# Decode attention, sixteen heads: V of the sixth pair loaded whole, a row selector built with one select, and the first load of K cut into 16 and 112 partitions

## The chip, the cores and the metric

The kernel runs on one core of one Trainium2 chip. The metric is device microseconds of one execution, as a median over runs. A profile of one execution is at hand too; its own time is given beside it below.

## The reference

One query row for each of 16 heads attends over 8192 keys; D is 256 and all data are bf16.

```python
B, H, Sq, Sk, D = 1, 16, 1, 8192, 256
scores = jnp.einsum("bhqd,bhkd->bhqk", q, k) * D ** -0.5
p = softmax(scores, axis=-1)
out = jnp.einsum("bhqk,bhkd->bhqd", p, v)
```

K and V are 64 MB each and each byte of them is used once.

## The kernel before, in words

The heads go in eight pairs, numbered 0 to 7. For one pair, head one lies on partitions 0 to 63 and head two on 64 to 127; each partition holds J = 128 consecutive keys of 256 elements, 64 KB. So the K of a pair is a transfer of 128 rows of 64 KB, 8 MB in all, and its V another. In the code `P` is 128, `HP` 64, `HJ` = J / 2 = 64, `NP` 8, `LAST` 7.

**The stream of loads.** All loads of K and V are issued by SP, one after the other, in the order that the string `ORDER` (line 17) gives: `k3` is K of pair 3, `v3` its V. A name in `parts` (line 100) is loaded in two halves of 32 KB a row, and the name with a plus is the second half. V of the last pair comes in five strips cut at `CUTS`. Line 136 issues each; lines 124 to 128 make SP wait first where the buffer is still in use. `kbuf` has room for two pairs, `vbuf` for one, so:

- a load of K of pair n waits until the K of pair n - 2 has been used by VectorE (semaphore `kd`) and GpSimd (`tp`);
- a load into the first half of `vbuf` waits until TensorE has used that half of the V before (semaphore `pa`);
- a load that reaches into the second half, a whole V among them, waits until TensorE has used all of the V before and made its total (semaphore `pr`). The test is `b <= HJ` in line 128.

SP runs its list in order, so a wait also holds up whatever comes later in `ORDER`. The semaphores `k0`, `k1`, `v` count the landing of whole transfers or of first halves (`k0` for even pairs, `k1` for odd), `kb`, `k7b`, `vb` that of second halves. Each transfer adds 16.

**The scores.** For each pair, GpSimd multiplies 24 keys of each half by q (line 215), ScalarE scales and sums these products (line 450), and VectorE does the other 40 keys of each half in one instruction per key (line 252). They start on a half of K when `k_waits` (line 149) and `side_wait` let them.

**The softmax and P times V.** When the scores of a pair are there, VectorE takes the maximum (`top`, line 234), TensorE turns it and spreads it (`turned`, line 292, `spread`, line 296), ScalarE makes the exponentials `E` (line 409). TensorE then multiplies `E` with the two halves of `vbuf`, 32 matmuls a half (`doubles`, line 319): it waits for semaphore `v`, does the first half, signals `pa`, waits for `vb`, does the second half, and `total` (line 307) signals `pr`. For the last pair only the first 92 keys go this way. TensorE then sums what it has so far over partitions (`gather`, line 341), adds the last 36 keys one by one (line 384), ScalarE and VectorE scale the row, and SP writes it out (lines 143 and 145).

**The small tables.** GpSimd builds `which` (2 x 128, in row r a one where the column belongs to head r) with a memset and two selects (lines 181 to 183), and then `ident` with a memset and one select. `which` is what TensorE needs, beside q, to spread the first q rows over the partitions (line 283).

Of the kernel before, what the change touches and what calls it, by code (L numbers as in the profile page):

```python
# [5 lines left out]
ALU = mybir.AluOpType  # L6
# [7 lines left out]
GRP = 3  # L14
CH = 8
SIDES = 2
ORDER = "k0 k0+ k1 v0 k2 v1 k3 v2 k4 v3 k5 v4 k6 k6+ k7 v5 v5+ k7+ v6 v6+ v7"
CUTS = (0, 64, 92, 112, 124)
LAST_PAIRED = 92
STRIP = 64  # L20
BLK = 32
ROWS = 98
AHEAD = {"sp": 2, "fin": 1, "rc": 2, "pr": 2, "pv": 2}
# [2 lines left out]
def bass_standalone__mha_softmax__decode_kernel(nc: bass.Bass, q: bass.AP, k: bass.AP, v: bass.AP, out: bass.AP):  # L26
    B, H, Sq, D = q.shape
    Sk = k.shape[2]
    P = 128
    NP = H // 2  # L30
    HP = P // 2
    J = Sk // HP
    HJ = J // SIDES
# [6 lines left out]
    HW = D // 2  # L40
    halves = ((0, 0), (BLK, HW))
    EW = 2 * J + BLK - 2
    LP = LAST_PAIRED
    LAST = NP - 1
    dt = k.dtype

    def pos(j):
        return j // BLK * (2 * BLK) + j % 2 * BLK + j % BLK // 2 * 2

    with contextlib.ExitStack() as ctx:  # L50

        def sb(name, shape, d):
            return ctx.enter_context(nc.sbuf_tensor(name, shape, d))
# [6 lines left out]
        def sem(name):  # L60
            if name not in sems:
                sems[name] = ctx.enter_context(nc.semaphore(name))
            return sems[name]
# [11 lines left out]
        which = sb("which", [2, P], dt)  # L75
# [9 lines left out]
        ones = small[:, 7:8]  # L85
        recip = small[0 : BLK + 2, 8 : 8 + NP]
        half = sb("half", [P, BLK + 2], FP32)
        negb = sb("negb", [P, 1], FP32)
        lsum = sb("lsum", [P, 1], FP32)
        ident = sb("ident", [P, P], FP32)  # L90
# [6 lines left out]
        spare = ps("spare", [P, 512])  # L97

        stream = []
        parts = {name: (0, HJ) for name in ("k0", "k6", "k7", "v5", "v6")}  # L100
        for name in ORDER.split():
            kind, n = name[0], int(name[1])
            if name == f"v{LAST}":
# [14 lines left out]
        def src(t, n):  # L118
            return t[0, 2 * n : 2 * n + 2].rearrange("h (p j) d -> (h p) (j d)", p=HP)

        @(lambda f: f(nc.sync))
        def _(sp):
            for kind, n, a, b, name in stream:
                if kind == "k" and n >= 2 and a == 0:
                    sp.wait_ge(sem("kd"), (n - 1) * NC)
                    sp.wait_ge(sem("tp"), (n - 1) * NG)
                elif kind == "v" and n >= 1 and a in (0, HJ):
                    sp.wait_ge(*((sem("pa"), n) if b <= HJ else (sem("pr"), n + 2)))
                if kind == "k" and n == 0 and a == HJ:
                    for late in ("k1", "kb", "k7b", "vb"):  # L130
                        sp.nop().then_inc(sem(late), 16)
                if kind == "k":
                    buf = kbuf[:, n % 2 * J * D :]
                else:
                    buf = vbuf
                sp.dma_start(buf[:, a * D : b * D], src(k if kind == "k" else v, n)[:, a * D : b * D]).then_inc(
                    sem(name), 16
                )
            sp.wait_ge(sem(stream[-1][-1]), 16)
            sp.wait_ge(sem("fin"), LAST + 1)  # L140
            flat = out.rearrange("b (n two) s d -> two (b n s) d", two=2)
            rows = qo[:, :].rearrange("t (n d) -> t n d", d=D)
            sp.dma_start(flat[:, 0:LAST, :], rows[:, 0:LAST, :]).then_inc(sem("o"), 16)
            sp.wait_ge(sem("fin"), LAST + 3)
            sp.dma_start(flat[:, LAST:NP, :], rows[:, LAST:NP, :]).then_inc(sem("o"), 16)
            sp.wait_ge(sem("o"), 32)
            sp.nop()

        def k_waits(e, h):
            e.wait_ge(sem("qb"), h + 1)  # L150
            e.wait_ge(sem("k0"), h // 2 * 16 + 16)
            e.wait_ge(sem("k1"), (h + 1) // 2 * 16 + 16)

        def side_wait(e, h, s):
# [4 lines left out]
        @(lambda f: f(nc.gpsimd))  # L159
        def _(pool):  # L160
            done = [0]

            def step(ins):
                done[0] += 1
                ins.then_inc(sem("pool"), 1)
                pool.wait_ge(sem("pool"), done[0])

            def keep(t, base, step_p, step_x, op, fill):
                step(
                    pool.affine_select(  # L170
                        out=t[:, :],
                        in_=t[:, :],
                        compare_op=op,
                        fill=fill,
                        base=base,
                        pattern=[[step_x, P]],
                        channel_multiplier=step_p,
                    )
                )

            step(pool.memset(which[:, :], 1.0))
            keep(which, 0, -HP, 1, ALU.is_ge, 0.0)
            keep(which, HP - 1, HP, -1, ALU.is_ge, 0.0)
            pool.nop().then_inc(sem("cb"), 1)
            for name, n in AHEAD.items():
                pool.nop().then_inc(sem(name), n)
            step(pool.memset(ident[:, :], 0.0))
            keep(ident, 0, 1, -1, ALU.not_equal, 1.0)
            step(pool.memset(ones, 1.0))
            step(pool.memset(half[:, :], 1.0))  # L190
            for c in (0, BLK):
                step(pool.memset(half[HP:P, c : c + 1], 0.0))
                step(pool.memset(half[0:HP, c + 1 : c + 2], 0.0))
            step(pool.memset(E[:, :], 0.0))
            for c in range(2):
                step(
                    pool.tensor_tensor(
                        out=sel[:, 2 * c : 2 * c + 2],
                        in0=ident[0:ROWS, c * BLK : c * BLK + 2],
                        in1=ident[0:ROWS, STRIP + c * BLK : STRIP + c * BLK + 2],  # L200
                        op=ALU.add,
                    )
                )
            pool.nop().then_inc(sem("cf"), 1)

            with pool.Fori(0, NP) as h:
                par = pool.snap(h % 2)
                with pool.Fori(0, SIDES) as s:
                    k_waits(pool, h)
                    side_wait(pool, h, s)  # L210
                    pool.nop().then_inc(sem("turn"), 1)
                    with pool.Fori(0, SG // 2) as i:  # L212
                        for b in range(2):
                            pool.wait_ge(sem("sp"), h * NG + s * SG + i * 2 + (b + 1))  # L214
                            pool.tensor_tensor(  # L215
                                out=prod[:, b * GRP * D : (b + 1) * GRP * D].rearrange("p (b d) -> p b d", b=GRP),
                                in0=kbuf[
                                    :, ds(par * (J * D) + s * (HJ * D) + i * (2 * GRP * D) + b * (GRP * D), GRP * D)
                                ].rearrange("p (b d) -> p b d", b=GRP),
                                in1=q_now[:, ds(par * D, D)].rearrange("p (b d) -> p b d", b=1).to_broadcast([P, GRP, D]),  # L220
                                op=ALU.mult,
                            ).then_inc(sem("tp"), 1)
# [58 lines left out]
        def _(pe):  # L281
# [33 lines left out]
            def doubles(a, b):  # L315
                for j in range(a, b, 2):
                    at = j // 2 % 2 * STRIP
                    x = pos(j)
                    ins = pe.matmul(  # L319
                        acc[at : at + STRIP, :],  # L320
                        lhsT=E[:, x : x + STRIP],
                        rhs=vbuf[:, j * D : (j + 2) * D],
# [33 lines left out]
            with pe.Fori(0, NP + 1) as h:  # L356
                par = pe.snap(h % 2)
                with pe.If(h > 0):
                    pe.wait_ge(sem("ex"), h)
                    pe.wait_ge(sem("v"), h * 16)  # L360
                    doubles(0, HJ).then_inc(sem("pa"), 1)
                    pe.wait_ge(sem("vb"), (h // (NP - 2) + h // LAST + h // NP) * 16 + 16)
                    doubles(HJ, LP)
                    with pe.If(h < NP):
                        doubles(LP, J)
                    total(h)
                with pe.If(h < NP):
                    pe.wait_ge(sem("m"), h + 1)
                    turned()
                    pe.wait_ge(sem("g"), h + 1)  # L370
                    spread()
                with pe.If(h < NP - 2):
                    qcast(back(h, -2), par)
                with pe.If(h > 0):
                    keep_running()
                    pe.wait_ge(sem("cm"), h)
                    pe.wait_ge(sem("fin"), h)
                    gather().then_inc(sem("pv"), 1)
# [124 lines left out]
```

## Time and profile before

| What | Value |
|---|---|
| Median of 3 runs | 316.98 us (316.96 to 317.62) |
| The profiled execution: its time | 317.37 us |
| Its span, from the first to the last instruction | 316.1 us |
| Bytes read from HBM | 134.23 MB |
| Busy: VectorE, GpSimd, ScalarE, TensorE | 225.6, 209.8, 194.6, 107.1 us |
| Share of the 16 DMA engines' span taken by SP's queue | 98.8% |

The span is 1.3 us shorter than the time of its own execution, and that execution took 0.39 us more than the median. In the page's second part each digit is a fortieth of the span, in tenths of busy time; the line for DMA is the mean over the 16 DMA engines. In the chain, each piece starts where the piece that released it ended; a DMA piece there runs from its issue to its landing, so it holds the time that the transfer stood in the queue behind others.

### The profile page before, as it was taken

The page shows a single profiled execution, that of the slowest core. Times are in us where ns is not written, and L with a number is a line of the kernel's source. Part 1 is how long each engine was busy: PE and PEld are TensorE (multiplying, and loading weights), DVE is VectorE, ACT ScalarE, POOL GpSimd, SP SyncE. Part 2 cuts the span into 40 slices and gives each one's busy share as a digit, 9 for nine tenths or more (in the row PEclk, how much of TensorE's full clock was granted, in tenths as well). Part 3 has the DMA queues.
Part 4 walks back from the last instruction along what each step waited for, and adds up shares of the span by engine and source line. Part 5 has one row for each costly group of instructions (what it writes and reads, how often), then busy time and mean ns, then how long its engine had stood idle before and what let it go on. Part 6 is the DMA issues. An engine that isn't in the chain of part 4 may idle for free.

```text
span 316.1 us, 7081 instructions
## 1 busy us (share of the span) xinstructions
PE 107.1 (34%) x718; PEld 46.8 (15%) x718; DVE 225.6 (71%) x1305; ACT 194.6 (62%) x840; POOL 209.8 (66%) x146
## 2 busy tenths in 40 slices
PE   0000000192005900069000790007700564258678
PEld 0000000041001400024000240002300122113335
DVE  0198989695596946969369692896989698969300
ACT  2066777766278653696537964468677967686541
POOL 3188888875486845858368582786888588868300
PEclk9999999997555785559755588555965558756779
DMA  8999999999999999999999999999999999999996
GB/s 333 402 460 456 473 398 398 489 440 398 398 398 531 398 398 398 531 398 398 489 440 398 398 531 398 398 398 464 398 464 398 464 398 464 398 464 406 456 400 267
DMA packets 3639, 134.25 MB, mean 425 GB/s; under 512 B 406, under 2 KB 438, under 8 KB 694
## 3 DMA queue, kind: packets, MB, share of 16 engines
q1 hardware_dynamic: 3620, 134.23, 98.8%
q8 instruction: 1, 0.02, 0.0%
q10 hardware_dynamic: 18, 0.01, 0.0%
HBM read 134.23 MB, written 0.01 MB: 425 GB/s over the span
## 4 chain that ended last, share of the span: by engine, by line
DMA 51%; POOL 16%; ACT 10%; PE 7%; issue 6%; ACTq 6%; POOLq 3%; SPq 0%
DMA kbuf<-in_k_dram 32%; DMA vbuf<-in_v_dram 19%; POOL prod L215 16%; ACT prod L450 8%; PE acc L319 6%; ACTq L450 4%; POOLq L215 2%; ACTq L446 2%; PE ob L384 1%; ACT E L409 0%; PE spare L330 0%; ACT comb L423 0%; POOLq L214 0%; POOLq L156 0%; POOLq L212 0%
## 5 line engine op out<-in xcount | busy, mean ns | idle before, releaser
L252 DVE SCALAR_TENSOR_TENSOR kbuf<-kbuf,qrow x640 | 219.9, 417 | 65.3 <-issue 65.3
L215 POOL TENSOR_TENSOR prod<-kbuf,q_now 128x768 f32 x128 | 207.0, 1639 | 83.5 <-ACT prod L450 46.3
L450 ACT ACTIVATE prod<-prod x384 | 155.3, 405 | 103.9 <-POOL prod L215 86.9
L319 PE MATMUL acc<-vbuf,E 128*64 128x512 bf16 x494 | 73.3, 468 | 15.7 <-DMA vbuf<-in_v_dram 12.7
L450 ACT ACTIVATION_READ_ACCUMULATOR prod<-prod x384 | 71.6, 186 | 0.0
L292 PE MATMUL mx<-ident,small 128*1 128x128 f32 x16 | 4.5, 380 | 176.2 <-DVE small L234 176.2
L252 DVE DVE_READ_ACCUMULATOR kbuf<-kbuf,qrow x640 | 52.8, 82 | 0.0
L319 PEld LDWEIGHTS acc<-vbuf,E 128*64 128x64 bf16 x494 | 33.0, 134 | 55.5 <-issue 25.8
L292 PEld LDWEIGHTS mx<-ident,small 128*1 128x1 f32 x16 | 0.7, 81 | 177.2 <-DVE small L234 177.2
L409 ACT ACTIVATE E<-S,negb 64x128 bf16 x16 | 13.9, 866 | 1.5 <-ACT negb L404 1.4
L330 PE MATMUL spare<-ident 128*128 128x512 f32 x16 | 14.7, 1016 | 0.1
L341 PE MATMUL ob<-comb,small 98*2 98x128 f32 x64 | 7.3, 373 | 9.9 <-ACT comb L423 9.9
L228 DVE RECIPROCAL small<-tot 34x1 f32 (+1 forms) x8 | 1.3, 159 | 10.8 <-PE tot L307 10.7
L423 ACT ACTIVATE comb<-acc 98x512 f32<-98x512 f32 x8 | 4.7, 593 | 6.2 <-PE tot L307 6.2
L409 ACT ACTIVATION_READ_ACCUMULATOR E<-S,negb 64x1 f32 x16 | 7.9, 494 | 0.0
L238 DVE TENSOR_REDUCE small<-mx 1x2 f32<-1x128 f32 x8 | 2.2, 279 | 7.0 <-PE mx L292 7.0
L341 PEld LDWEIGHTS ob<-comb,small 98*2 98x2 f32 x64 | 2.7, 99 | 22.0 <-ACT comb L423 21.0
L430 ACT ACTIVATE qo<-ob,small 2x128 f32 x14 | 4.9, 352 | 1.0 <-PE ob L341 0.9
L234 DVE TENSOR_REDUCE small<-S 128x1 f32 x8 | 2.3, 281 | 2.8 <-ACT prod L450 2.8
L296 PE MATMUL mx<-small 1*64 1x1 f32 x32 | 2.9, 244 | 3.0 <-DVE small L238 3.0
L330 PEld LDWEIGHTS spare<-ident 128*128 128x128 f32 x16 | 3.6, 279 | 1.4 <-issue 1.3
L283 PE MATMUL qrow<-qo,which 2*128 (+1 forms) x8 | 2.9, 391 | 2.6 <-DMA qo<-in_q_dram 2.4
(25 smaller groups left out, 19.9 us busy)
## 6 DMA issues: line engine op xcount, KB each, us to landing
kbuf<-in_k_dram SPq DMA_DIRECT2D x6, 4096.0 KB, 27.8
vbuf<-in_v_dram SPq DMA_DIRECT2D x5, 4096.0 KB, 23.7
vbuf<-in_v_dram SPq DMA_DIRECT2D x1, 1792.0 KB, 9.0
vbuf<-in_v_dram SPq DMA_DIRECT2D x1, 1280.0 KB, 11.7
vbuf<-in_v_dram SPq DMA_DIRECT2D x1, 768.0 KB, 13.1
vbuf<-in_v_dram SPq DMA_DIRECT2D x1, 256.0 KB, 13.3
kbuf<-in_k_dram SPq DMA_DIRECT2D x5, 44.1
vbuf<-in_v_dram SPq DMA_DIRECT2D x5, 27.9
```

What stands on the lines that cost most here:

```text
L215: pool.tensor_tensor(out=prod[:, b * GRP * D : (b + 1) * GRP * D].rearrange("p (b d) -> p b d", b=GRP), in0=kbuf[:, ds(par * (J * D) + s * ...
L252: ins = dve.scalar_tensor_tensor(out=col, in0=col, scalar=SCALE, in1=qrow[:, ds(par * 512, D)], op0=ALU.mult, op1=ALU.mult, accum_out=S[:, ...
L292: pe.matmul(mx[0:1, 0:P], lhsT=m[:, :], rhs=ident[:, :], start=True, stop=True).then_inc(sem("mT"), 1)
L319: ins = pe.matmul(acc[at : at + STRIP, :], lhsT=E[:, x : x + STRIP], rhs=vbuf[:, j * D : (j + 2) * D], start=(j < 4), stop=(j >= J - 4), s ...
L330: pe.matmul(spare[:, :].rearrange("p (b x) -> p b x", x=P), lhsT=ident[:, :], rhs=ident[:, :].rearrange("p (b x) -> p b x", b=1).to_broadc ...
L341: ins = pe.matmul(ob[row : row + 2, 0:HW], lhsT=sel[:, 2 * n : 2 * n + 2], rhs=comb[:, n * D + a : n * D + a + HW], start=(n == 0), stop=( ...
L384: ins = pe.matmul(ob[row : row + 2, 0:HW], lhsT=E[:, at : at + 2], rhs=vbuf[:, j * D + a : j * D + a + HW], start=False, stop=(j == J - 1) ...
L409: ins = act.activation(out=E[rows, 0 : 2 * J].rearrange("p (b two i t) -> p b i two t", b=J // BLK, two=2, t=2)[:, :, :, :, x], in_=S[rows ...
L423: act.activation(out=comb[:, :], in_=acc[0:ROWS, :], func=ACT.Copy).then_inc(sem("cm"), 1)
L430: ins = act.activation(out=qo[:, ds(i * D + a, HW)], in_=ob[row : row + 2, 0:HW], func=ACT.Copy, scale=recip[row : row + 2, ds(i, 1)],)
L446: with act.Fori(0, SG) as i:
L450: ins = act.activation(out=part, in_=part, func=ACT.Copy, scale=SCALE, accum_out=S[:, ds(par * J + s * HJ + i * GRP + b, 1)],)
```

## The change

Three things are done.

1. V of pair 5 (the sixth pair) is loaded in one transfer of 64 KB rows where it was two of 32 KB rows. Its one wait is that for a whole V, on `pr`. The threshold of TensorE's wait on `vb` loses the step that stood for this second half.
2. `which` is built with a memset of zeros and one select that puts a one where the row equals the head of the column. `ident` is built by the same helper, with the same operations as before.
3. The first half of K of pair 0, the first load of all, becomes two transfers on the same semaphore: partitions 0 to 15, and then partitions 16 to 127. The threshold of the wait on `k0` rises by 16.

```diff
-ORDER = "k0 k0+ k1 v0 k2 v1 k3 v2 k4 v3 k5 v4 k6 k6+ k7 v5 v5+ k7+ v6 v6+ v7"
+ORDER = "k0 k0+ k1 v0 k2 v1 k3 v2 k4 v3 k5 v4 k6 k6+ k7 v5 k7+ v6 v6+ v7"
...
+FIRST = 16
...
-        parts = {name: (0, HJ) for name in ("k0", "k6", "k7", "v5", "v6")}
+        parts = {name: (0, HJ) for name in ("k0", "k6", "k7", "v6")}
...
-                sp.dma_start(buf[:, a * D : b * D], src(k if kind == "k" else v, n)[:, a * D : b * D]).then_inc(
-                    sem(name), 16
-                )
+                rows = ((0, FIRST), (FIRST, P)) if (kind, n, a) == ("k", 0, 0) else ((0, P),)
+                for lo, hi in rows:
+                    sp.dma_start(
+                        buf[lo:hi, a * D : b * D], src(k if kind == "k" else v, n)[lo:hi, a * D : b * D]
+                    ).then_inc(sem(name), 16)
...
-            e.wait_ge(sem("k0"), h // 2 * 16 + 16)
+            e.wait_ge(sem("k0"), h // 2 * 16 + 32)
...
-            step(pool.memset(which[:, :], 1.0))
-            keep(which, 0, -HP, 1, ALU.is_ge, 0.0)
-            keep(which, HP - 1, HP, -1, ALU.is_ge, 0.0)
+            ones_where_zero(which, [[-1, 2], [0, HP]])
...
-            step(pool.memset(ident[:, :], 0.0))
-            keep(ident, 0, 1, -1, ALU.not_equal, 1.0)
+            ones_where_zero(ident, [[-1, P]])
...
-                    pe.wait_ge(sem("vb"), (h // (NP - 2) + h // LAST + h // NP) * 16 + 16)
+                    pe.wait_ge(sem("vb"), (h // LAST + h // NP) * 16 + 16)
```

The new helper:

```python
def ones_where_zero(t, pattern):
    step(pool.memset(t[:, :], 0.0))
    step(
        pool.affine_select(
            out=t[:, :], in_=t[:, :], compare_op=ALU.not_equal, fill=1.0,
            base=0, pattern=pattern, channel_multiplier=1,
        )
    )
```

More of the change, by code (lines that the diff above doesn't have):

```diff
@@ L166, in step @@
                 pool.wait_ge(sem("pool"), done[0])
-            def keep(t, base, step_p, step_x, op, fill):
+            def ones_where_zero(t, pattern):
+                step(pool.memset(t[:, :], 0.0))
                 step(
@@ L172, in keep @@
                         in_=t[:, :],
[L173 to L177, printed above, removed]
-                    )
-                )
-            step(pool.memset(which[:, :], 1.0))
-            keep(which, 0, -HP, 1, ALU.is_ge, 0.0)
-            keep(which, HP - 1, HP, -1, ALU.is_ge, 0.0)
+                        compare_op=ALU.not_equal,
+                        fill=1.0,
+                        base=0,
+                        pattern=pattern,
+                        channel_multiplier=1,
+                    )
+                )
+            ones_where_zero(which, [[-1, 2], [0, HP]])
             pool.nop().then_inc(sem("cb"), 1)
```

## The prediction

> **What bounds the kernel now.** I read the page first: the busy lines, the line of DMA slices, and the table of DMA queues.
>
> ```profile
> span 316.1 us, 7081 instructions
> ...
> DMA  8999999999999999999999999999999999999996
> ...
> q1 hardware_dynamic: 3620, 134.23, 98.8%
> ```
>
> No engine of the core is busy for more than 71% of the span, but the sixteen DMA engines are full in every slice except the first and the last. Then I asked for windows: the start in small pieces, and one long stretch of the middle (the last two columns are the share of the DMA engines and GB/s; a packet is counted whole where it starts, so a short window can show more than 1).
>
> ```profile
> core 0: us, PE busy (x) PEld busy (x) DVE busy (x) ACT busy (x) POOL busy (x), PEclk, DMA share, GB/s
> 0.00:1.72 1.72, 0.00 (x0) 0.00 (x0) 0.00 (x0) 0.34 (x1) 0.97 (x7) 1.00 0.00 0
> 1.72:1.82 0.10, 0.00 (x0) 0.00 (x0) 0.00 (x0) 0.10 (x1) 0.00 (x0) 1.00 0.15 46
> 1.82:2.02 0.20, 0.00 (x0) 0.00 (x0) 0.00 (x0) 0.20 (x1) 0.00 (x0) 1.00 6.59 1820
> 2.02:12.90 10.88, 0.60 (x2) 0.12 (x2) 0.00 (x0) 1.03 (x2) 1.82 (x11) 1.00 0.94 401
> 20.00:300.00 280.00, 94.13 (x572) 40.01 (x572) 219.52 (x1272) 186.19 (x816) 201.90 (x125) 0.70 1.00 432
> ```
>
> From 20 to 300 us the share is 1.00 at 432 GB/s: nothing in the core ever lets the queue run dry. The stream starts at 1.82. The chain of waits shows how it hangs together at both ends (start, length, what):
>
> ```profile
> 0.81 12.09 DMA kbuf<-in_k_dram
> ...
> 75.90 44.08 DMA kbuf<-in_k_dram
> ...
> 153.08 44.30 DMA kbuf<-in_k_dram
> ...
> 230.87 24.72 DMA vbuf<-in_v_dram
> 255.63 5.61 PE acc L319 x32
> 261.26 23.48 DMA vbuf<-in_v_dram
> 284.78 6.39 PE acc L319 x32
> 291.18 12.97 DMA vbuf<-in_v_dram
> 304.20 6.71 PE acc L319 x46
> 310.95 1.05 PE spare L330 x2
> 312.00 0.54 PE ob L341 x8
> 312.54 2.03 PE ob L384 x72
> 314.59 0.36 ACT qo L471
> ```
>
> Here the reader is to see two things. The end is set by the landing of the first half of the last V, 291.18 + 12.97 = 304.15, and 10.8 us of TensorE, ScalarE and output behind it. And every landing is set by the queue: a transfer lands when those ahead of it are through, however early it was issued. So the whole kernel is a pipe of fixed length. An edit pays, one for one, only if it starts the pipe sooner, shortens the sum of its transfers, or opens a gap in it.
>
> **The unit of the sum.** Halves first: from the landing of the first half of V5 (230.87 + 24.72 = 255.59) to that of V6 (261.26 + 23.48 = 284.74) three halves pass: 29.15 / 3 = 9.717 us each. Wholes: from K3 (75.90 + 44.08 = 119.98) to K5 (153.08 + 44.30 = 197.38) four pass, V2, K4, V3, K5: 77.40 / 4 = 19.35 us each. A half has 128 rows on 16 engines, eight rows an engine, so a 32 KB row takes 9.72 / 8 = 1.21 us of its engine, which moves 432 / 16 = 27 GB/s.
>
> **Part 1, V5 whole.** Two halves cost 2 x 9.717 = 19.43 us, a whole 19.35: the gain is 0.08 us of pipe. The bounds are 0 and 0.1, for both landings are read to hundredths. What it costs lies in waits, so these rows come next: SP's issues, and TensorE around V5.
>
> ```profile
> 227.38 0.20 PE L307 MATMUL tot<-lsum,half 128*34 128x1 f32 x2
> ...
> 230.50 0.33 SPq L136 DMA_DIRECT2D kbuf<-in_k_dram  x1
> 230.87 0.43 SPq L136 DMA_DIRECT2D vbuf<-in_v_dram  x1
> ...
> 265.34 5.33 PE L319 MATMUL acc<-vbuf,E 128*64 128x512 bf16 x32 [4.12 <-DMA vbuf<-in_v_dram]
> 270.51 0.20 PE L307 MATMUL tot<-lsum,half 128*34 128x1 f32 x2
> 277.37 0.59 PE L292 MATMUL mx<-ident,small 128*1 128x128 f32 x2 [6.66 <-DVE small L234]
> ...
> 284.78 0.64 PE L319 MATMUL acc<-vbuf,E 128*64 128x512 bf16 x2 [0.86 <-DMA vbuf<-in_v_dram]
> ```
>
> - SP's wait: the whole V5 waits for `pr`, given at 227.58 by the total of V4. SP only reaches V5 at 230.87, after waiting for K5 to be used up. The new wait is over 3.3 us before it is asked, and behind it in SP's list stands only the second half of K7, which now goes out one issue sooner.
> - TensorE: it can no longer start V5 at 255.63 with the first half; it waits for the whole, about 255.59 + 19.35 - 9.72 = 265.2. The first 32 matmuls then take what such a batch took, 5.33 to 6.39 us, so `pa` comes at 270.6 to 271.6 instead of 261.24, and SP issues the first half of V6 that late. The second half of K7 keeps the engines at work until 265.2 + 9.7 = 274.9, and an issue needs 1.82 - 0.81 = 1.01 us to its first data. So V6 must be issued by 273.9: a cover of 2.3 us at the worst batch.
> - TensorE's second batch ends at 275.9 to 278.0. The next thing it has to do is the turn at 277.37, so that is at most 0.7 late; TensorE idles 0.86 us before V6, which swallows it. The second half of V6, issued on `pr` by 278.3, is needed at about 283.6.
>
> So the whole of part 1 is -0.08 us.
>
> **Part 2, one select less.** GpSimd, and who waits for it:
>
> ```profile
> 1.07 0.63 POOL L170 TENSOR_SCALAR_AFFINE_SELECT which<-which 2x128 bf16<-2x128 bf16 x2
> 2.43 0.60 PE L283 MATMUL qrow<-qo,which 2*128 2x256 bf16 x2 [2.43 <-DMA qo<-in_q_dram]
> 14.33 3.23 POOL L215 TENSOR_TENSOR prod<-kbuf,q_now 128x768 f32 x2 [9.54 <-issue]
> ```
>
> Two selects took 0.63, so about 0.3 us go. But TensorE's first matmuls waited for q, not for `which` (done at 1.70), and GpSimd itself idles 9.54 us before its first product. Worth 0; without that cover it would be a gain of 0.3. A select over two dimensions could be slower than the plain one; the cover takes that in too.
>
> **Part 3, 16 rows ahead of 112.** This part has the only large unknowns. The first issue, the shortest one of the run, and one that directly follows another:
>
> ```profile
> L136 SPq DMA_DIRECT2D kbuf<-in_k_dram x1: 405/405/405, 0.8 to 0.8; - x1
> ...
> 314.97 0.28 SPq L145 DMA_DIRECT2D out_dram<-qo  x1
> ...
> 231.82 0.43 SPq L136 DMA_DIRECT2D kbuf<-in_k_dram  x1
> ```
>
> The first issue runs from 0.81 to 1.22 and the data start at 1.82, 0.60 later. A transfer with 2 rows was issued in 0.28, so with 16 rows at best 0.41 - 0.28 = 0.13 us go. If the 0.60 us of hand-over too shrank with the rows, to 16 / 128 of it, 0.53 us more would go: the far end of the gain is 0.66. The near end is 0: the trace has no 16-row load and an issue of 0.43 for 128 rows, so the count of rows may not matter. I take 0.13, since the two-row issue is the only row that is close in size.
>
> On the cost side, the second transfer is issued behind the first, by 1.22 + 0.05 + 0.43 = 1.70 at the latest, and has data 0.60 later, at 2.30. An engine has its first row of 1.21 us until 1.69 + 1.21 = 2.90 at the earliest, so there is no hole; without that cover it would cost the second issue, 0.48. The extra completion costs nothing that I can see: the halves against wholes above, with eight more rows an engine and a completion more, differ by 0.08 in all, so I take +0.01. All loads behind are issued 0.5 later, with 10 us of queue ahead.
>
> What the trace does not bear out is that sixteen neighbouring rows can be written at the full 432 GB/s. At full rate, one row an engine, they take 1.21 us and the pipe stays as long. The nearest rows: a 128-row load writes eight rows per engine's share of 27 GB/s. If a row group keeps just that share, sixteen rows have two shares and take 8 x 1.21 = 9.7, a loss of 8.5 us. Against that, the q load in the window 1.72 to 1.82 put 46 GB/s into two neighbouring rows, more than the one share of 27. It is a tenth of a microsecond and a few KB, which a buffer may have taken, but it is the only narrow write here, and I take it: no loss.
>
> [...]
>
> **The sum.** On the profiled execution: 317.37 - 0.08 - 0.13 + 0.01 = 317.17. That execution was 0.39 above the median of the runs, so against the median 316.98 - 0.20 = 316.78, say 316.8 us. A change of less than 0.2%, 0.63 us, is about what a measurement of this kernel cannot tell from none.
>
> **The rivals.**
>
> - *Narrow writes, slower.* Sixteen neighbouring rows share a part of the write side, and the first rows hold all sixteen engines, whose queues are in order. [...] If the 112 rows, seven to an engine, also fall unevenly, the loss grows towards the 8.5 of two shares: up to 325.3. It decides as soon as the first rows take more than 0.8 us longer than 1.21. For it: the eight rows per share above, and a pipe with no slack to hide it. Against it: the q load.
> - *The split does nothing.* The data start at 1.82 as before, and only 0.08 is left: 316.9.
> - *The hand-over shrinks too.* -0.66 - 0.08: 316.2, faster. Against it: 0.60 us after an issue is also what a mere latency would look like.
> - *V6 comes late.* If TensorE's first batch on V5 took over 8.7 us, the queue would dry up after K7, one for one. The rows say 5.3 to 6.4, so even 10 us would cost just 1.3: 318.1.
>
> **How the numbers follow.** The forecast has 0.47, the split that does nothing 0.10, the narrow writes 0.33 (0.20 near 320.4, 0.13 towards 325), the hand-over 0.07, a late V6 0.03. Within 0.2%: 0.47 + 0.10 = 0.57. Slower: 0.33 + 0.03 = 0.36. Faster: 0.07. The range runs from 316.2, the full hand-over, to 321.0, which takes in the loss of 3.6 and a little more; what lies beyond, 0.13 and some at the edges, is under 0.2. The forecast's own range is 316.3 to 317.4.
>
> **What would show it.** In the profile after, the first half of K0 should land at about 12.8 (12.90 before), the stream should show 432 GB/s from then on, and the first half of the last V should land near 303.9. [...] V5's matmuls should come as one batch of 64 from about 265, `which` with one select of some 0.3 us. A DMA share under 1.00 between 273 and 277 would show a late V6. The prediction is wrong if the first rows are slow, or if the start moves by more than 0.6 us.

## The result, and the profile after

| | Before | After |
|---|---|---|
| Median | 316.98 us (5 runs, 316.93 to 317.62) | 327.42 us (5 runs, 326.7 to 327.82) |
| The profiled execution: its time, its span | 317.37, 316.1 us | 326.7, 324.8 us |

The ratio is 1.0311, with a 95% interval of 1.0294 to 1.0327: the change costs 10.4 us by the medians. The profiled execution after is the fastest of its five, so the two profiled executions lie 9.3 us apart, and what makes up the other 1.1 no profile shows. The forecast was 316.8 us, no difference that can be measured, with a range from 316.2 to 321.0. It was wrong.

The page of the kernel after, its first line, the DMA slices and the rate in each slice, and then the rate in the kernel before:

```profile
span 324.8 us, 7080 instructions
...
DMA  8999998999999989989989999999999998999996
GB/s 134 291 291 448 500 404 387 500 404 396 500 396 412 492 387 460 444 387 500 404 387 500 404 396 500 396 412 428 444 420 428 452 460 383 444 444 404 444 401 253
```

```profile
GB/s 333 402 460 456 473 398 398 489 440 398 398 398 531 398 398 398 531 398 398 489 440 398 398 531 398 398 398 464 398 464 398 464 398 464 398 464 406 456 400 267
```

The line of DMA slices looks nearly the same as before. The rate does not: for the first three slices, 24 us, the engines are about as busy as before and move 134 to 291 GB/s, where they moved 333 to 460. Section 6 of the page has the landing of the 16 rows, 7.1 us after their issue at 0.74, so at 7.84:

```profile
kbuf<-in_k_dram SPq DMA_DIRECT2D x1, 512.0 KB, 7.1
```

Windows cut at the landings show the same (last two columns: share of the DMA engines, GB/s):

```profile
core 0: us, PE busy (x) PEld busy (x) DVE busy (x) ACT busy (x) POOL busy (x), PEclk, DMA share, GB/s
1.72:7.84 6.12, 0.60 (x2) 0.13 (x2) 0.00 (x0) 1.26 (x2) 1.84 (x11) 1.00 1.07 173
7.84:22.24 14.40, 0.00 (x0) 0.00 (x0) 0.00 (x0) 0.00 (x0) 0.00 (x0) 1.00 1.00 275
22.24:31.96 9.72, 0.00 (x0) 0.00 (x0) 7.94 (x47) 4.79 (x23) 7.20 (x5) 1.00 1.06 455
40.00:300.00 260.00, 86.52 (x536) 36.71 (x536) 206.45 (x1197) 173.60 (x758) 189.31 (x118) 0.68 1.00 433
```

Between 7.84 and 22.24 the share is 1.00 at 275 GB/s: each engine has a packet under way, but the packets get on slowly (1.5 to 3.2 us for a row of the 112, where a row takes 1.21 at 432 GB/s). From 22 us on, the rate is what it was. The chain of waits of the kernel after (start, length, what):

```profile
1.18 21.06 DMA kbuf<-in_k_dram
...
161.89 44.22 DMA kbuf<-in_k_dram
...
239.67 34.28 DMA vbuf<-in_v_dram
273.95 0.04 issue
273.99 8.63 PE acc L320 x64
...
282.68 20.41 DMA vbuf<-in_v_dram
...
309.38 12.72 DMA vbuf<-in_v_dram
...
322.14 1.08 PE ob L385 x32
...
323.24 0.36 ACT qo L472
```

The first half of the first K lands at 1.18 + 21.06 = 22.24 in place of 12.90: 9.34 us late. K of pair 5 lands at 206.11 in place of 197.38: 8.7 late. The span is 8.7 us longer too. So the whole loss in the trace is made before 22 us, and the pipe hands it on to the end. The 0.6 us between 9.34 and 8.7 lie between the landings of the first half of K and of K3, 107.08 us before (12.90 to 119.98) and 106.47 after (22.24 to 128.71). The loads between are the same, and two profiles of one kernel below differ there by more, 106.46 and 107.45, so this is a difference between executions.

The two small parts came out as worked out. V of the sixth pair runs as one batch of 64 matmuls, after its landing at 273.95. From the landing of K5 at 206.11 to there pass V4 (19.35), three halves of K (29.15) and V5, which leaves 19.34 us for it: 0.09 less than two halves. The first half of V6 is asked for at 279.20, 4.5 us before the second half of K7 is in (273.95 + 9.72 = 283.67):

```profile
279.20 31.09 SPq L139 DMA_DIRECT2D vbuf<-in_v_dram  x7
```

The select, and the matmuls that wait for q, in the timeline after:

```profile
1.17 0.28 POOL L174 TENSOR_SCALAR_AFFINE_SELECT which<-which 2x128 bf16<-2x128 bf16 x1 [0.24 <-POOL which L172]
...
3.98 0.60 PE L284 MATMUL qrow<-qo,which 2*128 2x256 bf16 x2 [3.98 <-DMA qo<-in_q_dram]
```

One select takes 0.28 us. The q rows are there 1.55 us later than before (2.43); nothing needs them before 22 us.

### The profile page after: what moved, and what is told of

It reads as the page before. It is cut to its first block, busy times and chain, and to the rows that moved or that the text cites. A ratio compares the mean times of both kernels' runs of the same rounds, so it can differ in the third digit from the quotient of the medians.

```text
span 324.8 us, 7080 instructions
## 1 busy us (share of the span) xinstructions
PE 103.9 (32%) x718; PEld 45.5 (14%) x718; DVE 225.6 (69%) x1305; ACT 195.1 (60%) x840; POOL 209.7 (65%) x145
## 4 chain that ended last, share of the span: by engine, by line
DMA 54%; POOL 15%; ACT 9%; issue 6%; ACTq 6%; PE 5%; POOLq 3%; SPq 0%
DMA kbuf<-in_k_dram 33%; DMA vbuf<-in_v_dram 21%; POOL prod L216 15%; ACT prod L451 8%; PE acc L320 4%; ACTq L451 4%; POOLq L216 2%; ACTq L447 1%; SPq L139 0%; ACT E L410 0%; PE ob L385 0%; ACT comb L424 0%; POOLq L215 0%; POOLq L159 0%; POOLq L213 0%
## 5 line engine op out<-in xcount | busy, mean ns | idle before, releaser
L320 PE MATMUL acc<-vbuf,E 128*64 128x512 bf16 x494 | 70.4, 454 | 21.9 <-DMA vbuf<-in_v_dram 18.8
L320 PEld LDWEIGHTS acc<-vbuf,E 128*64 128x64 bf16 x494 | 32.0, 130 | 59.8 <-issue 22.6
L399 ACT ACTIVATE q_now<-qrow (+1 forms) x8 | 3.1, 382 | 2.0 <-PE qrow L284 1.8
```

The costliest lines, as they stand in the source:

```text
L320: ins = pe.matmul(acc[at : at + STRIP, :], lhsT=E[:, x : x + STRIP], rhs=vbuf[:, j * D : (j + 2) * D], start=(j < 4), stop=(j >= J - 4), s ...
L399: act.activation(out=q_now[:, ds(at * D, D)], in_=qrow[:, ds(at * 512, D)], func=ACT.Copy).then_inc(sem("qb"), 1)
```

## The experiments

The theories, as they stood before the runs. *Shared write paths*, an assumption that no trace had shown: neighbouring partitions share a way into the memory, so rows that go to few of these ways are slow, and they hold up all engines, whose queues are in order. Against it: the loss belongs to the *start of the stream*, or to *one transfer more*, or to a transfer with *few rows*, or to the *read* of neighbouring rows in HBM, or in part to *V in one transfer*.

**The first K whole again.**

```diff
-rows = ((0, FIRST), (FIRST, P)) if (kind, n, a) == ("k", 0, 0) else ((0, P),)
+rows = ((0, P),)
...
-e.wait_ge(sem("k0"), h // 2 * 16 + 32)
+e.wait_ge(sem("k0"), h // 2 * 16 + 16)
```

> Only the split of the first load is undone; V of the sixth pair stays in one transfer and the row selection keeps its one select. If the split carries the whole loss, the time is that of the kernel before less the 0.08 us that the prediction gave to V in one transfer: 316.9 us. If V in one transfer, or the select, has a part in the 10.4 us, what is left of the loss shows here: any time over 317.6, the slowest run of before.

Measured: 317.29 us beside 317.52 of the kernel before, ratio 0.9998 (0.9977 to 1.0019). The loss is gone. The runs spread further, though: seven lie at 316.7 to 317.4 and five at 317.9 to 320.0. In the kernel that cuts along the keys, below, on the same chip, four of ten lie at 319.4 to 320.5; the kernel before has one of 23 above 319 there. That is taken up below. In its chain the first half of K lands at 0.74 + 12.12 = 12.86:

```profile
0.74 12.12 DMA kbuf<-in_k_dram
...
152.46 44.26 DMA kbuf<-in_k_dram
230.22 34.34 DMA vbuf<-in_v_dram
```

**The split alone**, in the kernel before, with V in two halves and two selects.

> The kernel before with the split of the first load alone; V of the sixth pair stays in two halves and the selector in two selects. The extra loads by themselves cost 3.1 us over full rate for the 16 rows and 6.2 us for the 112. If the split is the whole loss, 9.3 us more than before and little spread, about 326.7. If V in one transfer has a share of its own in the 10.4 us, this kernel is faster than the changed one by that share, about 1 us.

Measured: 327.32 us beside 317.36, ratio 1.032 (1.03 to 1.0339). The changed kernel had 1.0311. So the split carries all of the loss, and the other two parts have none of it, within 0.2%. In its chain the first half of K lands at 1.25 + 21.59 = 22.84, 9.9 us late:

```profile
1.25 21.59 DMA kbuf<-in_k_dram
```

**Two transfers, cut along the keys.**

```diff
-rows = ((0, FIRST), (FIRST, P)) if (kind, n, a) == ("k", 0, 0) else ((0, P),)
+cols = ((0, 8), (8, HJ)) if (kind, n, a) == ("k", 0, 0) else ((a, b),)
...
-buf[lo:hi, a * D : b * D], src(k if kind == "k" else v, n)[lo:hi, a * D : b * D]
+buf[:, lo * D : hi * D], src(k if kind == "k" else v, n)[:, lo * D : hi * D]
```

> The first half of the first K still comes in two transfers, but cut along the keys: 8 keys and then 56 keys, each over all 128 rows. Shared write paths (neighbouring rows share a way into the memory, and the engines' queues are in order): all rows are written side by side again, so no loss, about 317 us and the half landed at about 12.9 us. A cost of starting the stream with two transfers: the loss stays, 8 to 10 us, so 325 to 327.

Measured: 317.37 us beside 317.52, ratio 1.0015 (0.9989 to 1.004). The half is there at 1.20 + 12.40 = 13.60, 0.7 us later than in one transfer, so it gains nothing, but the 9 us are not there. Two transfers at the start of the stream are not the cause.

```profile
1.20 12.40 DMA kbuf<-in_k_dram
```

**The same cut, in the middle of the stream.**

```diff
-rows = ((0, FIRST), (FIRST, P)) if (kind, n, a) == ("k", 0, 0) else ((0, P),)
+rows = ((0, FIRST), (FIRST, P)) if (kind, n, a) == ("k", 6, 0) else ((0, P),)
...
-e.wait_ge(sem("k0"), h // 2 * 16 + 32)
+e.wait_ge(sem("k0"), h // 2 * 16 + 16 + h // 6 * 16)
```

> The cut into 16 and 112 rows is made at the first half of the seventh K, some 225 us into a running stream; the first K is whole. Shared write paths: the same rows meet the same paths, so 8 to 10 us more again, 325 to 327. If the loss belongs to the start of the stream, 316.9. If it is a fixed cost of one transfer more, it must already be hidden by a full queue: under 317.5.

Measured: 328.38 us beside 317.52, ratio 1.0325 (1.0288 to 1.0362). In its chain K5 still lands at 197.12 (196.72 with the first K whole), and V5 at 275.65 in place of 264.56:

```profile
152.56 44.56 DMA kbuf<-in_k_dram
230.61 45.04 DMA vbuf<-in_v_dram
```

A window of the same kernel over the stretch between the two:

```profile
core 0: us, PE busy (x) PEld busy (x) DVE busy (x) ACT busy (x) POOL busy (x), PEclk, DMA share, GB/s
223.00:237.00 14.00, 4.61 (x46) 2.35 (x40) 7.04 (x42) 7.14 (x32) 6.49 (x4) 0.84 0.94 267
```

The same picture as at the start: the engines nearly full, at 267 GB/s. The loss goes with the rows, not with the start. From K5 to V5 it is 78.53 us in place of 67.84, so 10.7 more; why that is 1.4 above the loss at the start, no run here tells.

**64 and 64 rows.**

```diff
-FIRST = 16
+FIRST = 64
```

> The first half of the first K is cut into rows 0 to 63 and 64 to 127. If the loss comes from a transfer of very few rows, it should nearly go, since each has half of all rows: under 318. Shared write paths: 64 neighbouring rows reach only a part of them, and at half of the paths each transfer takes as long as the whole one, 9.72 us twice in place of once: +9.7, 326.6 us. [...]

Measured: 328.08 us beside 317.52, ratio 1.0327 (1.0299 to 1.0355); the half lands at 1.35 + 22.41 = 23.76, 10.9 us late. Two transfers of half the rows take some 10 us each, as long as one with all rows. So it is not the small number of rows in the first transfer that costs the time.

```profile
1.35 22.41 DMA kbuf<-in_k_dram
```

**Sixteen rows by themselves**, in three ways. The first K is whole; ahead of it go 16 extra rows into the buffer of V, and V's first load waits for them.

```diff
+sp.dma_start(vbuf[0:16, 0 : HJ * D], src(k, 0)[0:16, 0 : HJ * D]).then_inc(sem("x"), 16)
 for kind, n, a, b, name in stream:
+    if kind == "v" and n == 0:
+        sp.wait_ge(sem("x"), 16)
```

> The first K is whole again; ahead of everything SP loads 16 rows of the first K once more, into partitions 0 to 15 of the buffer of V, which is loaded over them later. So the cost of a 16-row transfer stands by itself. Full rate, one 32 KB row an engine: 1.21 us, the first half of K lands at 12.9 + 1.2 = 14.1 us. [...]

Every eighth partition: `vbuf[0:121:8, ...]`.

> The same 16 rows of K, but written to every eighth partition (0, 8, 16 to 120) in place of 0 to 15. [...]

Every eighth row of HBM: `src(k, 0)[0:121:8, ...]`.

> Partitions 0 to 15 are written as in the first of these four, but with every eighth row of K from HBM in place of 16 neighbouring ones. [...]

Measured, in this order, beside 317.41 us: 321.11, ratio 1.0118 (1.0097 to 1.0139); 319.36, 1.0063 (1.0042 to 1.0084); 321.38, 1.0124 (1.0103 to 1.0145). The chains, one fence each, give the landing of the first half of K: 17.15, 15.48 and 17.43, where 12.86 is the value without extra rows.

```profile
1.18 15.97 DMA kbuf<-in_k_dram
```

```profile
1.39 14.09 DMA kbuf<-in_k_dram
```

```profile
1.18 16.25 DMA kbuf<-in_k_dram
```

So, by the landings, 16 rows cost 4.3 us in neighbouring partitions and 2.6 us in partitions that lie eight apart, from the same rows of HBM; other rows of HBM into the same partitions, 4.6. At full rate it would be 1.21. By the medians the three cost 3.7, 2.0 and 4.0 us, in the same order. So what decides here is which partitions are written: 4.3 and 4.6 us for 0 to 15, 2.6 for every eighth.

The traces also have the time of each packet, and each row of 32 KB is one packet (128 packets for each of the eleven loads of 32 KB rows in the kernel before). In the first half of K of the kernel before, a row takes 1.21 to 1.3 us from the second row of each engine on, and 1.3 to 2.2 for each engine's first. The 16 neighbouring rows take 3.2 to 4.5 us each (3.0 to 4.4 in the changed kernel), the 16 rows eight apart 1.8 to 2.5, and the rows of the two transfers of 64, after the first, 2.4 to 2.6.

**The 112 rows by themselves**, in the same way.

> The same with rows 16 to 127, 112 of them, seven an engine, ahead of the whole first half. Even use of the paths: 7 x 1.21 = 8.49 us, the half of K lands at 21.4. [...]

Measured: 331.62 us beside 317.41, ratio 1.0446 (1.0424 to 1.0467). The half lands at 27.55, so 112 rows took 14.7 us: 6.2 more than 8.49. Its packets are slow throughout: each of the seven rows of an engine takes 1.6 to 2.8 us.

```profile
1.18 26.37 DMA kbuf<-in_k_dram
```

The books close by the landings: 4.3 - 1.2 = 3.1 for the 16 rows and 6.2 for the 112 make 9.3; the changed kernel's first half landed 9.34 late, that of the split alone 9.9. By the medians the same sum is 2.5 + 5.7 = 8.2, less than the 10.0 to 10.4 of the two kernels with the split, so the close fit holds for these profiles and not for every run. Either way some two thirds of the loss lies in the large transfer, which looks harmless. Which engine gets which of the 112 rows the trace does not tell, so why they are slow is not shown.

**V in one transfer, and the spread of the runs.** Three more kernels, on one chip. The first is the one with the first K whole, once more.

> The kernel with the first K whole and V of the sixth pair in one transfer, once more, on the same chip as its three neighbours here. In its first comparison the runs lay in two groups, 316.7 to 317.4 and 318 to 320 us. If the upper group comes from the late issue of V of the seventh pair (3.3 us ahead of need in the profile with the loss), it is here again. If it belonged to that chip, all runs lie within 316.7 to 317.6.

Measured: 317.41 us beside 317.36, ratio 1.0003 (0.9991 to 1.0015), nine runs from 316.8 to 317.8 and two at 318.4 and 318.5; the kernel before had two over 318 among 17. The runs up to 320 did not come back.

The profile with the first K whole was, the first time, that of the run of 320.0 us. In it the first half of V6 is asked for at 270.97, 3.3 us before the second half of K7 is in (264.56 + 9.72 = 274.28):

```profile
270.97 32.56 SPq L139 DMA_DIRECT2D vbuf<-in_v_dram  x7
...
274.45 20.66 DMA vbuf<-in_v_dram
```

Even so the second half of V6 lands at 274.45 + 20.66 = 295.11 and not at 264.56 + 29.15 = 293.71, three halves behind V5. In the changed kernel it lands at 282.68 + 20.41 = 303.09, just these three halves behind 273.95. So 1.4 us of what that run took longer do lie at V6, although it was asked for in time.

In the next one the first half of the seventh V waits for `pr`, until all of the sixth is used.

```diff
-sp.wait_ge(*((sem("pa"), n) if b <= HJ else (sem("pr"), n + 2)))
+sp.wait_ge(*((sem("pa"), n) if b <= HJ and n != 6 else (sem("pr"), n + 2)))
```

> As the kernel with the first K whole, but the first half of V of the seventh pair waits until TensorE is through with all of V of the sixth: issue at about 274.5 in place of 271.0, when the queue runs empty at about 274. With 1.01 us from issue to first data, as at the start of the program, the pipe has a gap of about 1.6 us: 318.5. If a transfer that meets an empty queue needs more until it runs at full rate (the first half of K took 2.4 us more than its 9.7 from issue to landing), about 3 us: 319.5 or more.

Measured: 319.89 us (318.5 to 321.3) beside 317.36, ratio 1.0082 (1.0059 to 1.0105). Its timeline and windows:

```profile
274.13 28.98 SPq L139 DMA_DIRECT2D vbuf<-in_v_dram  x7
...
286.17 5.13 PE L320 MATMUL acc<-vbuf,E 128*64 128x512 bf16 x32 [2.24 <-DMA vbuf<-in_v_dram]
```

```profile
core 0: us, PE busy (x) PEld busy (x) DVE busy (x) ACT busy (x) POOL busy (x), PEclk, DMA share, GB/s
274.35:275.05 0.70, 0.00 (x0) 0.00 (x0) 0.70 (x7) 0.41 (x4) 0.30 (x1) 1.00 0.00 0
275.05:275.70 0.65, 0.00 (x0) 0.00 (x0) 0.65 (x7) 0.65 (x3) 0.53 (x1) 1.00 2.59 756
```

The issue is at 274.13, the first data come between 275.05 and 275.70 (the first packet at 275.09), and the share is 0 before: this is what a dry queue looks like. The expectation had a gap of 1.6 us; in this profile, that of a run of 318.84 us, the second half of V6 lands 1.4 us late (295.84, where three halves behind V5 are 265.25 + 29.15 = 294.40). Why the median lost more, no profile shows. In the neighbour with the shorter wait the same half is asked for 2.5 us earlier, and TensorE does not miss it:

```profile
271.61 30.02 SPq L139 DMA_DIRECT2D vbuf<-in_v_dram  x7
...
284.99 6.52 PE L320 MATMUL acc<-vbuf,E 128*64 128x512 bf16 x32 [0.79 <-DMA vbuf<-in_v_dram]
```

So the rival of a late V6 is a real mechanism, and the changed kernel stays clear of it in its profile. The third loads the sixth V ahead of the last K.

```diff
-k6 k6+ k7 v5 k7+ v6
+k6 k6+ v5 k7 k7+ v6
```

> As the one above, but V of the sixth pair is loaded before the first half of the last K and not between its halves, so that the seventh V is issued with some 10 us more of queue ahead. Late issue as the cause of the upper group: it vanishes, 316.7 to 317.4, or up to 0.9 us more because the last K lands 10 us later, at 265, where VectorE took it up at 263.4 before. No such cause: the groups are as in the neighbour.

Measured: 319.21 us beside 317.36, ratio 1.0053 (1.0037 to 1.0069). More than the 0.9 us expected: the last K is wanted earlier than it now comes, and TensorE's turn of the maximum for the last pair starts at 280.12 where its neighbour has 277.66. It does not tell where the runs up to 320 came from, and since they did not come back, their cause stays open. That V in one transfer costs something in part of the executions is not excluded.

## Why the prediction was wrong

*The step that failed* is in part 3: "it is the only narrow write here, and I take it: no loss". The q load of a few KB in a tenth of a microsecond was taken as the nearest row for a load of 512 KB. It moved 46 GB/s into two neighbouring rows; sixteen rows of 32 KB moved 512 KB in 4.3 us, some 120 GB/s. The prediction itself named a buffer as the way in which the q row could mislead. The runs showed in its place 4.3 us for the 16 rows by themselves, where the prediction took 1.21, and 14.7 for the 112, where full rate has 8.49. What both cost is shown, and for the 16 that it hangs on the partitions written (2.6 us eight apart); why the 112 are slow is not. The other bound, eight rows per engine's share, pointed the right way, and rested on loads of the disputed size.

*The rival was right in its direction and too small.* "Narrow writes, slower" had 0.33. That neighbouring rows are slow the runs show; that they share a part of the write side stays its assumption. No run shows the 3.6 us behind its 320.4 and behind the end of the range: the 16 rows lost 3.1 (4.3 less 1.2) in its place. The mis-sized term is the 112 rows: for them the rival let the loss grow "towards the 8.5 of two shares" in all, and they alone lost 6.2. So the sum of 9.3 in the trace lies above its far end, and the range, cut at 321.0, held only the loss of the 16 rows.

*What held:* the pipe has no slack, and a loss at its start arrives at the end, 9.3 to 8.7 us of it in the profile; V in one transfer gains 0.08 of pipe in the profile (0.09 by its landings), which no comparison of times here could tell from nothing; the select is covered, as q is what TensorE waits for; `pa` and `pr` come in time in the profile after. The gains from a shorter first issue did not come: the issue of 16 rows took 384 ns, against 405 for 128, so 0.02 us in place of the 0.13 of the sum. The first packet of K starts at 1.76, 1.02 us after the start of that issue, as before (0.81 to 1.83). So the hand-over did not shrink with the rows.

```profile
L139 SPq DMA_DIRECT2D kbuf<-in_k_dram x1: 384/384/384, 0.7 to 0.7; - x1
```

## What to carry to other kernels

When a kernel is bound by its loads, a load over fewer than all partitions has to be priced by a measured load over the same partitions, and the remainder of a cut like that too (here 4.3 us for 16 neighbouring rows and 14.7 for the other 112, where all 128 have 9.72). A cut along the free dimension, in which each transfer has all 128 rows, came here without a loss (317.37 us beside 317.52). In the profile, put GB/s beside the DMA share: the loss lay here where the share was 1.00 at 275 GB/s, in place of 432. And a row that carries a decision must resemble the disputed thing in size, not only in shape.

## What the runs showed of the hardware

- Sixteen rows of 32 KB cost the stream 4.3 us in neighbouring partitions, 2.6 us eight partitions apart, and 1.21 us would be their part of a full-width load. 112 rows cost 14.7 us, more than the 9.72 of all 128.
- A 64-row load takes about as long as a 128-row one of the same row size: two of 64 had landed 22.41 us after the second issue, one of 128 rows 12.09 us after its issue, with rows of 2.4 to 2.6 us against 1.21.
- The DMA engines had a busy share of 1.00 at 275 GB/s while 112 rows were loaded, and the same share at 432 to 433 GB/s with full-width loads.
- A transfer that meets an empty queue has its first data about 1 us after the start of its issue: 1.02 at the start of the program (0.74 to 1.76), for 16 rows as for 128, and 0.96 in the middle (274.13 to 275.09).
